# Wd loaded early into the rows of Wk and Wv, row normalisation allowed on GpSimd, and a new unit order, in a linear-attention block with a bilinear MLP

## The chip, the cores and the metric

The kernel runs on one core of one Trainium2 chip. The metric is the device time in microseconds (us). Kernels that are compared were run on the same chip in the same rounds as the kernel before.

## The reference, cut to what matters

```python
x = A_x                                     # 1 x 2048 x 640, bf16
h  = x + attn(layernorm(x)) ; out = h + mlp(layernorm(h))

def attn(x):                                # H = 32 heads of 20
    q, k, v = split(x @ wqkv)
    phi(t)  = concat(softmax(t @ w_phi), softmax(-(t @ w_phi)))
    kv = phi(k)^T v ;  z = sum over s of phi(k)
    o  = (phi(q) kv) / (phi(q) z + 1e-6)
    return o @ wo
def mlp(x):                                 # F = 1536
    return ((x @ w_gate) * (x @ w_up)) @ w_down
```

There are 16 row tiles of 128 rows. Each is normalised, transposed and projected to K and V; all sixteen must have gone into `kv` before any `o` is made.

## The kernel before

The program is a graph of named units. Unit `xn5` normalises row tile 5, `K5` and `V5` are its projections, `KV5` its key-value product, `wd0` a piece of the load of `w_down`. A table gives each unit a key and, sometimes, an alternative engine. A list scheduler orders the units on each engine with estimated costs; each engine then runs its own list strictly in order, with semaphores between the engines. So a unit that waits holds up everything behind it on its engine.

The statistics of a row tile give a mean `mv`, a reciprocal deviation `rs` and a bias `nb = -mean * rs`. VectorE normalises with mean and deviation; ScalarE needs the bias instead. The bias is made on GpSimd, for every tile from 2 on:

```python
for t in tl:
    if t > 1:
        G.op("pool", "L1n%d" % t, lambda e, t=t: e.tensor_scalar(
            out=T["nb"][:, t:t + 1], in0=T["mv"][:, t, 0:1], scalar1=T["rs"][:, t:t + 1], scalar2=-1.0,
            op0=ALU.mult, op1=ALU.mult), 0.2, LP, [rs_b[t], mv_b[t]], [nb_b[t]], 10 * t - 25)
# ... cut ...
def xn(e, eng="dve", t=t, xb=xb):
    if eng == "act":
        return e.activation(out=rev(xb), in_=..., func=AF.Identity,
                            scale=T["rs"][:, t:t + 1], bias=T["nb"][:, t:t + 1])
    return e.tensor_scalar(out=rev(xb), in0=..., scalar1=T["mv"][:, t, 0:1], scalar2=T["rs"][:, t:t + 1],
                           op0=ALU.subtract, op1=ALU.mult)
G.op("dve", "xn%d" % t, xn, 0.5, LD, [x_b[t], mv_b[t], rs_b[t], nb_b[t]], [xb], 10 * t - 22,
     alts=[] if t < 2 else [("act", act_c(640, True), LA)])
```

The unit lists `nb_b[t]` among what it reads whichever engine runs it. VectorE's form does not use the bias and waits for it all the same.

The cost that the scheduler assumes for any GpSimd operation of n columns, and the load of Wd, which lies over the first twelve of the fifteen row tiles of the weights of Q, K and V and so waits for the last projection:

```python
def pool_c(n):
    return 0.183 + 0.0017 * n
# ... cut ...
for k in range(4):
    dma("sp", "wd%d" % k, lambda k=k: T["Wd"][:, 3 * k:3 * k + 3, :], ..., 492, [wd_b[k]], key=310,
        after=lastproj)
```

The softmax here doesn't subtract the row's maximum and nothing guards it: scores larger than these inputs give would overflow.

## Time and profile before

| what | before |
|---|---|
| median, and range of 3 runs | 282.76 us, 282.46 to 282.84 |
| span of the profiled execution | 281.1 us |
| first real matmul starts, last ends | 5.59 us, 278.53 us |
| TensorE busy from 15.5 to 50 us | all of 34.5 us |
| normalisation on VectorE, ScalarE, GpSimd | 11, 5, 0 tiles |

The main lines of the page are in the prediction. Beside them, the views of single source lines show what the units in question cost; each gives engine, operation, tiles and count, then the shortest, median and longest duration in ns, and the first and last start in us. Here are the normalisation on VectorE and on ScalarE, the bias on GpSimd, and the only other row operation of 640 columns that GpSimd does, a product of two inputs.

```profile
L442 DVE TENSOR_SCALAR xn<-x_all,mv,rs x11: 589/597/605, 5.3 to 41.6; 128x640 bf16<-128x640 bf16 x11
...
L440 ACT ACTIVATE xn<-x_all,nb,rs x5: 910/921/959, 14.0 to 38.8; 128x640 bf16<-128x640 bf16 x5
...
L421 POOL TENSOR_SCALAR nb<-mv,rs x14: 262/267/268, 13.2 to 40.8; 128x1 f32<-128x1 f32 x14
...
L599 POOL TENSOR_TENSOR scratch<-scratch,sm x10: 1271/1272/1277, 88.6 to 218.2; 128x640 bf16<-128x640 f32 x10
```

### The profile page before, as it was taken

How to read it: one execution, taken by the hardware profiler on the slowest of the kernel's cores; microseconds unless marked ns; L12 is line 12 of the kernel's file. 1: busy time of each engine (PE TensorE's matmuls, PEld its weight loads, DVE VectorE, ACT ScalarE, POOL GpSimd, SP SyncE). 2: the span in 40 equal slices, each digit the busy share in tenths (PEclk: the TensorE clock that was granted, in tenths of full speed). 3: DMA queues.
4: the chain of work that ended last, by engine and by line, in shares of the span. 5: the costliest groups of instructions: out<-in, count | busy, mean ns of one | idle time of the engine just before them, and what ended most of it. 6: DMA issues, size and time to landing. Idle time of an engine off the chain costs nothing.

```text
span 281.1 us, 5047 instructions
## 1 busy us (share of the span) xinstructions
PE 274.9 (98%) x2058; PEld 182.7 (65%) x2075; DVE 176.8 (63%) x357; ACT 109.6 (39%) x217; POOL 61.3 (22%) x78
## 2 busy tenths in 40 slices
PE   7899999999999999999999999999999999999996
PEld 3677777876556688765555675545675554587874
DVE  5899986542588798855888974338725452341532
ACT  3799876846785742112311301303200203330200
POOL 6017998873002102202012000010110200000000
PEclk9999999999999999999999999999999999999999
DMA  7923276990011692232111342010141230000001
GB/s 211 369 56 74 53 131 113 313 372 8 0 26 31 153 261 48 41 79 49 25 23 26 70 106 60 0 23 2 25 97 47 40 32 23 0 2 23 26 34 60
DMA packets 43479, 21.98 MB, mean 78 GB/s; under 512 B 34624, under 2 KB 42176, under 8 KB 43456
## 3 DMA queue, kind: packets, MB, share of 16 engines
q1 hardware_dynamic: 42080, 20.02, 28.9%
q10 hardware_dynamic: 1376, 1.64, 1.9%
q8 instruction: 16, 0.26, 0.4%
q14 instruction: 7, 0.06, 0.1%
HBM read 11.00 MB, written 2.62 MB: 48 GB/s over the span
## 4 chain that ended last, share of the span: by engine, by line
PE 95%; DMA 2%; DVE 1%; issue 0%; ACTq 0%; ACT 0%; POOL 0%; DVEq 0%
PE ps L652 36%; PE ps L671 19%; PE ps L473 16%; PE ps L610 8%; PE ps L534 8%; PE ps L567 4%; PE ps L513 4%; DMA scratch<-in_A_wqkv_dram 2%; PE ps L389 1%; PE ps L370 0%; PE ps L451 0%; DVE x_all L614 0%; DVE ev L660 0%; DVE st L620 0%; ACTq L274 0%
## 5 line engine op out<-in xcount | busy, mean ns | idle before, releaser
L652 PE MATMUL ps<-xnT,Wgu 128*128 128x512 bf16 (+1 forms) x587 | 106.4, 335 | 0.7
L652 PEld LDWEIGHTS ps<-xnT,Wgu 128*128 128x128 bf16 x600 | 58.1, 98 | 41.7 <-DVE ev L660 0.6
L657 ACT ACTIVATE scratch<-ps 128x512 bf16<-128x512 f32 (+1 forms) x60 | 30.7, 512 | 117.4 <-PE ps L652 98.5
L660 DVE TENSOR_TENSOR ev<-ps,scratch 128x512 bf16<-128x512 f32 (+1 forms) x60 | 33.6, 579 | 34.5 <-ACT scratch L657 18.7
L671 PE MATMUL ps<-Wp,ev 128*128 128x320 bf16 (+2 forms) x396 | 53.5, 295 | 0.0
L671 PEld LDWEIGHTS ps<-Wp,ev 128*128 128x128 bf16 x396 | 38.0, 98 | 14.1
L473 PE MATMUL ps<-Wp,xnT 128*128 128x320 bf16 x320 | 45.9, 299 | 0.0
L504 POOL TENSOR_TENSOR ev<-ev,SR 128x1280 bf16<-128x1280 bf16 x16 | 37.4, 2358 | 9.5 <-ACT SR L502 9.5
L473 PEld LDWEIGHTS ps<-Wp,xnT 128*128 128x128 bf16 x320 | 30.7, 98 | 11.2
L599 POOL TENSOR_TENSOR scratch<-scratch,sm 128x640 bf16<-128x640 f32 x10 | 12.7, 1273 | 94.9 <-DVE sm L596 91.7
L683 DVE SCALAR_TENSOR_TENSOR Wp<-ps,rs,x_all 128x640 bf16<-128x640 f32 (+3 forms) x18 | 14.5, 808 | 30.0 <-PE ps L671 30.0
L497 DVE TENSOR_REDUCE SR<-ev 128x64 f32<-128x1280 bf16 x16 | 23.3, 1475 | 6.2 <-ACT ev L494 6.1
L610 PE MATMUL ps<-Wo,scratch 128*128 128x320 bf16 x160 | 24.0, 299 | 0.0
L543 ACT ACTIVATE eqT<-ps 128x512 bf16<-128x512 f32 x40 | 21.4, 598 | 6.2 <-PE ps L534 6.2
L494 ACT ACTIVATE ev<-ps 128x640 bf16<-128x640 f32 x32 | 21.6, 713 | 4.2 <-PE ps L473 3.6
L534 PE MATMUL ps<-xnT,Wp 128*128 128x512 bf16 x96 | 21.9, 379 | 0.2
L610 PEld LDWEIGHTS ps<-Wo,scratch 128*128 128x128 bf16 x160 | 15.6, 98 | 7.0 <-issue 0.2
L614 DVE TENSOR_TENSOR x_all<-ps,x_all 128x640 bf16<-128x640 f32 x16 | 12.9, 813 | 7.8 <-PE ps L610 7.8
L534 PEld LDWEIGHTS ps<-xnT,Wp 128*128 128x128 bf16 x100 | 9.6, 98 | 10.3
L567 PE MATMUL ps<-KVm,eqT 128*128 128x154 bf16 (+1 forms) x192 | 15.7, 221 | 0.0
L567 PEld LDWEIGHTS ps<-KVm,eqT 128*128 128x128 bf16 x192 | 13.0, 98 | 4.0
L624 POOL TENSOR_SCALAR ln<-mv 128x1 f32<-128x1 f32 x16 | 3.3, 210 | 49.4 <-DVE mv L623 47.3
(59 smaller groups left out, 204.4 us busy)
## 6 DMA issues: line engine op xcount, KB each, us to landing
out_dram<-Wp SPq DMA_DIRECT2D x15, 160.0 KB, 1.8
x_all<-in_A_x_dram SPq DMA_DIRECT2D x6, 320.0 KB, 10.0
Wgu<-in_B_w_up_dram SPq DMA_DIRECT2D x5, 384.0 KB, 7.7
Wgu<-in_B_w_gate_dram SPq DMA_DIRECT2D x5, 384.0 KB, 6.1
Wp<-in_B_w_down_dram SPq DMA_DIRECT2D x4, 480.0 KB, 5.2
scratch<-in_A_wqkv_dram ACTq DMA_DIRECT2D x2, 320.0 KB, 5.5
Wo<-in_A_wo_dram SPq DMA_DIRECT2D x1, 480.0 KB, 9.0
xnT<-xn SPq DMA_TRANSPOSE x28, 2.7
```

The lines of the kernel that those rows point to most:

```text
L473: ins = e.matmul(pb(b, hb)[:, 0:320], lhsT=T["xnT"][:, NC - 1 - c, P * t:P * (t + 1)], rhs=T["Wp"][:, kind, c, 320 * hb:320 * (hb + 1)], s ...
L494: G.op("act", "Kx%d_%d" % (t, s), lambda e, s=s, b=b, ek=ek: e.activation(out=T["ek"][:, ek.slots[0], s, :].rearrange("p (b n) -> p b n", ...
L497: G.op("dve", "Ks%d" % t, lambda e, ek=ek, sr=sr: e.tensor_reduce(out=T["SR"][:, sr.slots[0], 0, :], in_=T["ek"][:, ek.slots[0], :, :].rea ...
L504: G.op("pool", "Kn%d" % t, lambda e, ek=ek, sr=sr: e.tensor_tensor(out=T["ek"][:, ek.slots[0], :, :].rearrange("p s (h f) -> p (s h) f", f ...
L534: ins = e.matmul(pb(b)[:, 0:n], lhsT=T["Wp"][:, 0, i, P * c:P * (c + 1)], rhs=T["xnT"][:, NC - 1 - i, o0:o0 + n], start=(i == 0), stop=(i ...
L543: G.op("act", "Qx%d_%d_%d" % (q, c, s), lambda e, s=s, c=c, o0=o0, n=n, b=b: e.activation(out=T["eqT"][:, s, c, o0:o0 + n], in_=pb(b)[:, 0 ...
L567: ins = e.matmul(pb(b, y)[:, 22 * h0:22 * (h0 + j1 - j0)], lhsT=T["eqT"][:, s, c, P * t:P * (t + 1)], rhs=T["KVm"][:, OFF[s, c] + j0:OFF[s ...
L610: ins = e.matmul(pb(b, hb)[:, 0:320], lhsT=T["oT"][:, oT.slots[0], c, :], rhs=T["Wo"][:, c, 320 * hb:320 * (hb + 1)], start=(c == 0), stop ...
L652: ins = e.matmul(pb(b)[:, 0:n], lhsT=T["Wgu"][:, gu, c, P * ft:P * (ft + 1)], rhs=T["xnT"][:, NC - 1 - c, o0:o0 + n], start=(c == 0), stop ...
L657: G.op("act", "g%d_%d" % (bi, ft), lambda e, pg=pg, gt=gt, n=n: e.activation(out=T["gt"][:, gt.slots[0], 0:n], in_=pb(pg)[:, 0:n], func=AF ...
L660: o_ = G.op("dve", "u%d_%d" % (bi, ft), lambda e, pu=pu, gt=gt, hh=hh, ft=ft, n=n: e.tensor_tensor(out=T["hh"][:, hh.slots[0], ft, 0:n], i ...
L671: ins = e.matmul(pb(b, hb)[:, 0:w], lhsT=T["hh"][:, hh.slots[0], ft, P * tt:P * (tt + 1)], rhs=T["Wd"][:, ft, c0 + w * hb:c0 + w * (hb + 1 ...
```

## The change

It has three parts. Wd is laid out so that ten of its twelve row tiles lie over Wk and Wv, and may load while Q is being computed. Normalisation gets GpSimd as a third choice. And a new table of keys was searched with these freedoms; it puts tiles 4, 5 and 11 on GpSimd, 7 and 14 on ScalarE, the rest on VectorE.

```diff
+WDP = [(0, 3), (3, 5), (5, 8), (8, 10), (10, 12)]
 TUNED = {}                                  # about 170 lines of keys, replaced as a whole; cut
+def wdc(f):
+    return 5 + f if f < 10 else f - 10
@@ bias
-            if t > 1:
+            if t not in TPE:                # TPE = (0, 1, 2, 3)
@@ normalisation
-             alts=[] if t < 2 else [("act", act_c(640, True), LA)])
+             alts=[] if t in TPE else [("act", act_c(640, True), LA), ("pool", pool_c(640), LP)])
@@ load of Wd
-    for k in range(4):
-        dma("sp", "wd%d" % k, ... T["Wd"][:, 3 * k:3 * k + 3, :], ..., 492, [wd_b[k]], key=310, after=lastproj)
+    for k, (f0, f1) in enumerate(WDP):
+        own = lastproj if f0 >= 10 else [o for o in projs if o.name[0] == ("K" if f0 < 5 else "V")]
+        dma("sp", "wd%d" % k, ... T["Wd"][:, wdc(f0):wdc(f0) + WDN[f0], :], ..., 164 * (f1 - f0), [wd_b[k]], key=310, after=own)
@@ down matmul
-    rhs=T["Wd"][:, ft, ...]
+    rhs=T["Wd"][:, wdc(ft), ...]
@@ scheduler's estimate of a load: two constants changed; place of the output rows moved; cut
```

Every matmul stays, in shape and in number.

## The prediction

> **What bounds the kernel now.** I read the page first: busy time by engine, the 40 slices, then the costliest groups. TensorE is busy nearly all of the time; no other engine passes two thirds.
>
> ```profile
> PE 274.9 (98%) x2058; PEld 182.7 (65%) x2075; DVE 176.8 (63%) x357; ACT 109.6 (39%) x217; POOL 61.3 (22%) x78
> PE   7899999999999999999999999999999999999996
> PEclk9999999999999999999999999999999999999999
> ```
>
> The first slice and the last are the only ones with room, and the clock is full throughout. But a busy TensorE is not yet a TensorE at its own rate, so I took the cadence from the chain that ended last, in order of time.
>
> ```profile
> 8.41 0.73 PE ps L370 x10
> ...
> 15.52 15.21 PE ps L473 x112
> 30.73 1.36 PE ps L513 x24
> ...
> 195.25 3.24 PE ps L652 x15
> ...
> 265.45 13.08 PE ps L671 x108
> ```
>
> 15.21/112 is 0.136 us for a matmul of 320 columns, 3.24/15 is 0.216 us for 512 columns, 1.36/24 is 0.057 us for the small ones of the key-value product. Elsewhere in that chain 256 columns go at 0.109 us (1.64/15), six numerator matmuls in 0.36 us, one fold of six in 0.32 us, a transpose of five in 0.28 us.
>
> Now the work, counted in the source. Gate and up: 360 of 512 columns and 240 of 256, 77.8 + 26.2 = 104.0 us. Down: 372 x 0.136, plus 12 of 192 and 12 of 128 columns (about 0.083 and 0.056 each), 52.2. K and V: 320 x 0.136 = 43.5. Q: 100 x 0.216 = 21.6. Output projection: 160 x 0.136 = 21.7. Numerators 32 x 0.36 = 11.4, key-value 16 x 0.68 = 10.9, folds 10 x 0.32 = 3.2, transposes 9 x 0.28 = 2.5. The sum is **271.0 us**. The first real matmul starts at 5.59 us and the last ends at 278.53, which is 272.9 us. So in the whole stream TensorE loses about **1.9 us**, 0.2 of it a warm-up matmul. The waits of TensorE say where:
>
> ```profile
> PE ps L370 <- DMA scratch<-in_A_wqkv_dram: 1.4, 2, 1.1
> PE ps L349 <- DVE zero L344: 1.2, 1, 1.2
> ```
>
> Its one long wait is for the second piece of Wk (until 8.41 us); after that the list has nothing. The chain shows one stretch of VectorE and GpSimd, 219.66 to 222.69 us, but the timeline has 19 matmuls of 512 columns running from 219.46 on, so it is no hole. The limits, then: a head of 5.6 us (launch, first DMA), 1.9 us of loss, 271.0 us of matmuls, and a tail of 281.1 - 278.5 = 2.5 us (last combination and output write).
>
> **What the Trainium skill says.** "Perfetto Trace Analysis", Identifying the Most-Contended Engine, warns that matmul busy share is a bad measure of headroom. This case agrees that it can't be used alone: one 512-column matmul is recorded as 379 ns but follows the last by 216. Hence the sum by cadence. "TensorE: Matmul & The Clock Gate", Back-to-back issue gap, gives N/2.4 + 2.5 ns for an isolated matmul and 131 ns at N=512 as sustained. The trace has 216 ns, which is the formula and not the sustained figure. "GPSIMD Engine Reference", 3.1 Elementwise, puts GpSimd at about 1.8 to 2.6 cycles an element, the upper one for two inputs; the two-input product of 640 columns on GpSimd took 1.27 us here (820 ns on VectorE), in line. "DMA: Bandwidth & Descriptors", Issuing engines are not separate DMA queues, says that all transfers share the same 16 engines, so moving the Wd load moves what it may disturb.
>
> **The change, part by part.** Every matmul stays: same shapes, same count. So TensorE's 271.0 us stay, and only the 1.9 us, the head and the tail can move.
>
> (1) Wd. Before, four pieces of 480 KB are issued at 94.9 to 96.8 us, because Wd takes the place of Wq, Wk and Wv and must wait for the last Q matmul. They move at 340 to 400 GB/s and land at about 103 us.
>
> ```profile
> 94.84 1.36 PE ps L610 x10
> ...
> 115.88 6.52 PE ps L671 x48
> ```
>
> The first down matmul comes at 115.88 us, so the load was hidden with 13 us to spare. Now ten of twelve row tiles go into the rows of Wk and Wv and may start after the last K and V projection, about 62 to 67 us, and the last two after Q. The loads of Wgu and Wo stop near 63 us (372 GB/s in the slice to 63, then 8, 0, 26), so the lanes are free. At some 370 GB/s the 1.6 MB need 4.4 us (an estimate) and end before the first transposes of o near 79 us. Worth on the path: **0**. It frees the time from 95 to 103 us of DMA traffic; the transposes there take 2.9 us against a usual 2.6 to 2.7, hidden too.
>
> (2) Normalisation on GpSimd. The new order puts three of the sixteen (tiles 4, 5, 11) on GpSimd and two on ScalarE (five before); VectorE keeps eleven. ScalarE saves 3 x 0.92 = 2.8 us; GpSimd gains 3 x about 1.2 = 3.6 (an estimate between the page's one-input rate, 640 x 1.8 / 1.2 GHz = 0.96 us, and the measured 1.27) and loses two bias operations of 0.27. These engines are crowded where it happens, 14 to 42 us:
>
> ```profile
> 14.00:28.00 14.00, 14.00 (x112) 10.24 (x110) 14.00 (x32) 13.51 (x31) 6.10 (x7) 1.00 0.31 66
> 28.00:42.00 14.00, 14.00 (x141) 11.03 (x139) 13.03 (x21) 11.53 (x27) 14.00 (x14) 1.00 0.45 90
> ```
>
> (Columns: TensorE, weight loads, VectorE, ScalarE, GpSimd busy, clock, DMA.) VectorE and GpSimd are full, and yet TensorE is busy for all 14.00 us. Relief of an engine that TensorE does not wait for is worth **0**. It helps the search for an order, not this time.
>
> (3) The new order of units. At the start the DMA issues up to the sixth x load are the same, so the second Wk piece should land at about 8.4 us again. In front of that wait TensorE has the same amount to do (two weight transposes, one x transpose, one fold). Behind it the fold of chunk 0 now comes first, so its copy on ScalarE comes later, and the copies of chunks 0, 3 and 2 (0.70 us each) queue there in front of K's third chunk. With the trace's durations I get about 0.45 us of gaps between 8.4 and 13.6 us, where before has 7.11 us elapsed less 6.76 us of matmuls by cadence = 0.35 us up to 15.52. Cost: **0 to +0.2 us**.
>
> In the middle I looked at the tight places. K15 to its key-value product: about 6.3 us of chain (two exponentials 1.36, reduction 1.48, logarithm and exponential 0.53, product on GpSimd 2.36, hand-overs 0.5) against 7.7 us of matmuls placed between. The end of O0 to the first gate matmul: some 6.4 us (addition 0.82, statistics 1.1, centring 0.82, transpose 2.7, hand-overs) against 7.1 us placed between, where the old order left 7.8. Both hold, the second with 0.7 us only. I add **+0.1** for such places.
>
> At the end the last piece is 128 columns wide, not 192: the combination takes 343 ns in place of 418, and the output of 32 KB about as long as 48 KB (1.6 and 1.5 us). Worth **-0.1**.
>
> Sum: 0 + 0 + 0.1 + 0.1 - 0.1, about 0.1 us, less a little for the likelihood that an order was kept because it ran well. From 282.76 I stay at **282.7 us**.
>
> **The rivals.** First, the start gains: if the order cut all the loss, it would save at most 1.7 us (1.9 less the warm-up), giving 281.1. For it: all the loss is there. Against it: the wait is for a transfer whose issue is unchanged. Second, a new wait in TensorE's in-order queue: a fixed order tuned on estimates may block on a late transpose or a GpSimd product. GpSimd is full from 28 to 42 us and now gets more there; a slip of 1 to 3 us would give 284 to 286. Against it: the old order, made the same way, lost nothing after 15.5 us. Third, the early Wd load collides with a transpose or the last Wgu pieces. Those are first read near 96 us, 30 us later, so it should be hidden; time 282.7. Fourth, freed ScalarE speeds things: no TensorE wait names ScalarE; 282.7.
>
> **Range and chances.** To be faster by 2% means 5.7 us, which is more than loss, idle start and tail offer without removing a matmul: 0.01. To be slower by 2% needs 5.7 us of new stalls: 0.02. The rest, 0.97, is within. Range 281.7 (half of the early loss gone) to 283.8 (one new stall of about a microsecond).
>
> **What will show it.** Right: TensorE about 98% busy, the last matmul ending near 278.5 us, no wait of TensorE after 16 us, the same wait for the Wk piece until about 8.4. Wd issues near 64 to 69 us and one near 97, none of them in the list of waits. GpSimd busy about 64 us, ScalarE about 107. Wrong: if the Wk piece lands at another time; if TensorE's list names a transpose, a GpSimd product or a Wd transfer; if normalisation on GpSimd takes far over 1.3 us and K4, K5 or K11 wait for it.

## The result, and the profile after

| what | before | after |
|---|---|---|
| median, and range of 4 runs each | 282.68 us, 282.46 to 282.84 | 285.33 us, 285.2 to 285.44 |
| ratio, with 95% interval | | 1.0094, 1.0077 to 1.0112 |
| span of the profiled execution | 281.1 us | 283.7 us |
| first real matmul starts, last ends | 5.59, 278.53 us | 5.57, 281.26 us |
| normalisation on VectorE, ScalarE, GpSimd | 11, 5, 0 tiles | 11, 2, 3 tiles |

Ratios here and below are the mean time of one kernel's fast runs over that of the other's of the same rounds, so not quite the ratio of the medians that are quoted. The changed kernel is slower by 0.9%: within 2%, but 1.5 us beyond the predicted range.

From the first matmul to the last it takes 275.7 us, where before took 272.9: 2.8 us more. The tail behind the last matmul is 0.13 us shorter (2.44 against 2.57), so nearly all of the 2.6 us of span is TensorE's. The busy line of the page, against the first line of the prediction:

```profile
PE 276.2 (97%) x2075; PEld 182.4 (64%) x2075; DVE 179.4 (63%) x359; ACT 107.3 (38%) x214; POOL 66.2 (23%) x77
```

GpSimd is at 66.2 us where about 64 was predicted. That looks like a near hit and is not one, as the last part shows. The waits of TensorE have new entries; each line gives who was waited for, then us in total, times, and the longest.

```profile
PE ps L377 <- DMA scratch<-in_A_wqkv_dram: 1.3, 2, 0.9
...
PE ps L480 <- ACT ev L245: 1.2, 1, 1.2
PE ps L480 <- DVE ev L245: 0.8, 2, 0.5
```

The first is the old wait for the second piece of Wk. The other two are K and V projections (line 480) waiting for a copy out of PSUM (`ps`, where the results of the matmuls land), on ScalarE once and on VectorE twice; two waits of 0.2 us on ScalarE are left out here. By the order of units in the source the four late ones are K6, K4, K9 and K12, and each waits for a slot of PSUM, not for its own row tile. Neither says GpSimd. The table by stage says where: columns as in the prediction, the busy us of TensorE, weight loads, VectorE, ScalarE and GpSimd, then clock, DMA share and GB/s.

```profile
14.00:28.00 14.00, 12.59 (x98) 8.74 (x96) 11.96 (x24) 11.16 (x25) 10.59 (x9) 1.00 0.31 69
28.00:42.00 14.00, 13.55 (x128) 10.30 (x127) 11.76 (x24) 9.77 (x26) 14.00 (x11) 1.00 0.31 61
42.00:50.00 8.00, 7.64 (x78) 5.95 (x76) 6.64 (x7) 5.22 (x11) 8.00 (x8) 1.00 0.75 122
```

Before, the third of these stages was

```profile
42.00:50.00 8.00, 8.00 (x87) 6.44 (x85) 5.27 (x5) 5.39 (x13) 5.98 (x3) 1.00 0.73 113
```

and the first two stand in the prediction. TensorE loses 1.41, 0.45 and 0.36 us in these stages, 2.2 us together, and nothing that matters behind them. VectorE and ScalarE are less busy than before (11.96 against 14.00, 11.16 against 13.51, from 14 to 28 us): they wait too. GpSimd is busier, 10.59 against 6.10. The remaining 0.6 us hides in the records: a matmul of 320 columns is recorded as 299 ns but follows the last by 136, so each of the four gaps is some 0.16 us longer than it looks.

The chain that ended last, in order of time (start, us, what), confirms it. Before, it stays on TensorE from 15.52 us on, but for the short stretch near 220 us that the prediction tells of; now it lies almost wholly on GpSimd from 17.41 to 46.31 us.

```profile
17.41 0.74 POOL nb L428 x3
18.15 5.00 POOL xn L449 x2
23.15 0.24 POOL nb L428
23.39 9.26 POOL ev L511 x4
...
33.36 2.48 POOL xn L449
...
47.58 2.88 PE ps L480 x20
```

Two normalisations take 5.00 us. The view of that source line, with the median in the middle:

```profile
L449 DVE TENSOR_SCALAR xn<-x_all,mv,rs x11: 552/598/607, 5.3 to 47.9; 128x640 bf16<-128x640 bf16 x11
L449 POOL TENSOR_SCALAR xn<-x_all,mv,rs x3: 2499/2507/2525, 18.1 to 33.3; 128x640 bf16<-128x640 bf16 x3
```

The same operation takes 0.60 us on VectorE and **2.51 us on GpSimd**, twice the 1.2 that the prediction and the 1.27 that the scheduler's formula (0.183 + 0.0017 x 640) gave it. How this reaches TensorE is in the timeline around 23 us (start, us, engine, line, operation, and in brackets the idle time before it and its releaser):

```profile
18.13 5.02 POOL L449 TENSOR_SCALAR xn<-x_all,mv,rs 128x640 bf16<-128x640 bf16 x2
...
23.13 0.27 POOL L428 TENSOR_SCALAR nb<-mv,rs 128x1 f32<-128x1 f32 x1
...
23.43 0.92 ACT L447 ACTIVATE xn<-x_all,nb,rs 128x640 bf16<-128x640 bf16 x1 [2.42 <-POOL nb L428]
...
24.25 0.68 ACT L245 ACTIVATE ev<-ps 128x640 bf16<-128x640 f32 x1
...
24.99 1.53 PE L480 MATMUL ps<-Wp,xnT 128*128 128x320 bf16 x10 [1.23 <-ACT ev L245]
```

The bias for tile 7, a quarter of a microsecond of work, stands in GpSimd's list behind the two long normalisations. ScalarE idles 2.42 us for it, because the normalisation of tile 7 is next in *its* list. A copy out of PSUM stands behind that, and TensorE needs the slot which that copy frees. Three engines in a row, and the list of TensorE's waits names only the last hand. The later stalls are of the same family. VectorE's reduction at 38.50 us waited 0.77 us for a product on GpSimd, and the copy behind it, at 40.02, released TensorE at 40.94. VectorE's normalisation at 43.31 us waited 2.51 us for a bias that stood behind products on GpSimd, and the copy behind that, at 46.62, released TensorE at 47.58 us. VectorE's own operations are not slower beside the long ones: its normalisation has a median of 598 ns (597 before), its reduction a mean of 1476 ns (1475 before). So it was late, not slowed.

That is the reading of one trace. What it does not tell is which part is the cause: the long operation, the crowded list, the bias, or the order as such.

### The profile page after: what moved, and what is told of

Same layout as the page of the kernel before. It is cut to its first block, busy times and chain, and to the rows that moved or that the text cites. A ratio compares the mean times of both kernels' runs of the same rounds, so it can differ in the third digit from the quotient of the medians.

```text
span 283.7 us, 5057 instructions
## 1 busy us (share of the span) xinstructions
PE 276.2 (97%) x2075; PEld 182.4 (64%) x2075; DVE 179.4 (63%) x359; ACT 107.3 (38%) x214; POOL 66.2 (23%) x77
## 4 chain that ended last, share of the span: by engine, by line
PE 85%; POOL 10%; DMA 2%; ACT 1%; DVE 0%; issue 0%; ACTq 0%; DVEq 0%
PE ps L660 37%; PE ps L679 18%; PE ps L618 8%; PE ps L541 8%; PE ps L480 7%; POOL ev L511 7%; PE ps L575 4%; POOL xn L449 3%; DMA scratch<-in_A_wqkv_dram 2%; PE ps L520 2%; PE ps L396 1%; POOL nb L428 1%; ACT ev L501 1%; PE ps L377 0%; DVE ev L245 0%
## 5 line engine op out<-in xcount | busy, mean ns | idle before, releaser
L660 PE MATMUL ps<-xnT,Wgu 128*128 128x512 bf16 (+1 forms) x600 | 108.6, 336 | 0.0
L480 PE MATMUL ps<-Wp,xnT 128*128 128x320 bf16 x320 | 46.6, 299 | 2.2 <-ACT ev L245 1.2
L504 DVE TENSOR_REDUCE SR<-ev 128x64 f32<-128x1280 bf16 x16 | 23.4, 1476 | 5.4 <-ACT ev L501 4.6
L607 POOL TENSOR_TENSOR scratch<-scratch,sm 128x640 bf16<-128x640 f32 x8 | 10.2, 1272 | 60.4 <-DVE sm L604 60.4
L541 PE MATMUL ps<-xnT,Wp 128*128 128x512 bf16 x100 | 23.0, 379 | 0.0
```

Of the source, the lines that this page charges most:

```text
L480: ins = e.matmul(pb(b, hb)[:, 0:320], lhsT=T["xnT"][:, NC - 1 - c, P * t:P * (t + 1)], rhs=T["Wp"][:, kind, c, 320 * hb:320 * (hb + 1)], s ...
L504: G.op("dve", "Ks%d" % t, lambda e, ek=ek, sr=sr: e.tensor_reduce(out=T["SR"][:, sr.slots[0], 0, :], in_=T["ek"][:, ek.slots[0], :, :].rea ...
L541: ins = e.matmul(pb(b)[:, 0:n], lhsT=T["Wp"][:, 0, i, P * c:P * (c + 1)], rhs=T["xnT"][:, NC - 1 - i, o0:o0 + n], start=(i == 0), stop=(i ...
L660: ins = e.matmul(pb(b)[:, 0:n], lhsT=T["Wgu"][:, gu, c, P * ft:P * (ft + 1)], rhs=T["xnT"][:, NC - 1 - c, o0:o0 + n], start=(c == 0), stop ...
```

## The experiments

**Theory T**: the two-operation form of `TENSOR_SCALAR` takes 2.51 us on GpSimd, and this alone, through GpSimd's in-order list, delays TensorE. **Rivals**: the new order is slow by itself (R1); the early load of Wd disturbs something (R2); GpSimd is slow only because other engines use the memory at the same time (R3). In the expectations, "Theory A" is T, B is R1 and C is R2. In the experiments that move a unit, all other lists keep their order, and the unit goes to the same point in time on another engine's list:

```python
def _move(names, eng):                      # order[e]: the finished list of engine e
    for n_ in names:
        o_ = G.by[n_]
        order[o_.eng].remove(o_)
        o_.eng = eng
        insert o_ into order[eng] before the first unit with a later start
```

### 1. Only the normalisations, put into the old kernel

```diff
 # kernel before
+_move(["xn4", "xn5", "xn11"], "pool")
```

> The kernel before with only the normalisations of tiles 4, 5 and 11 put on GpSimd, at the same places in time. Theory A: GpSimd is full from 22 to 48 us there too, so 2.5 us each push the key-value products and bias operations back: 283.5 to 286 us with new TensorE waits between 20 and 50 us. Theories B and C: 282.7, no new wait.

Measured: 285.52 us (285.39 to 285.62) against 282.51, ratio 1.0107 (1.009 to 1.0124). The old order, with the old load of Wd, loses 3.0 us by this one part. Its list of TensorE's waits:

```profile
PE ps L473 <- DMA xnT<-xn: 1.5, 1, 1.5
...
PE ps L389 <- ACT SR L502: 0.7, 1, 0.7
```

The long operations run at 17.91 us, 5.01 us for two, and here TensorE waits for a transposed tile. So the loss needs neither the new order nor the early Wd, and R1 and R2 are not needed for a loss of this size. Where TensorE ends up waiting depends on the order; how much is lost is about the same.

### 2. The normalisations taken off GpSimd in the new kernel, to VectorE

```diff
 # kernel after
+_move(["xn4", "xn5", "xn11"], "dve")
```

> The changed kernel with the three normalisations (tiles 4, 5, 11) moved from GpSimd back to VectorE, everything else in the same order. Theory A (GpSimd needs 2.5 us for each where 1.2 was reckoned, and the bias operations and key-value products queue behind): the stalls of TensorE at 23.5 and 40 to 47 us go, 282.4 to 283.2 us. Theory B (the new unit order itself has the stalls): stays at 285.0 to 285.5. Theory C (the early Wd load disturbs): stays at 285.3.

Measured: 284.32 us (283.86 to 285.28) against 282.51, ratio 1.0069 (1.0044 to 1.0095). A quarter of the loss goes, not all: less than T had led me to expect (282.4 to 283.2 us). The waits for copies out of PSUM are gone, but there is a new one:

```profile
PE ps L480 <- DMA xnT<-xn: 1.0, 1, 1.0
```

It lies at 46 us. VectorE was busy for all of 14.00 us from 14 to 28 us in this run and runs late. The chain that ended last leads back from that tile to VectorE, and lies on it nearly all the way from 35.0 back to 11.9 us. This is not a clean undo: it puts 1.8 us on an engine that has no room there, and so it does not separate T from R1. A cleaner test had to keep the lists and change only the duration (run 7).

### 3. What the operation costs, form by form

Sixteen extra GpSimd operations were added at the end of the kernel before, two of each form, each waiting for the last one. They ran from 226.7 to 257 us, where VectorE is much less busy (4.14 of 13.00 us from 232 to 245) than in the crowd.

```diff
 # kernel before, end of GpSimd's list; M, X: 128 x 640 bf16; MR, XC: the same in five chunks, MR reversed
+2 x tensor_scalar(out=MR, in0=XC, mean, rstd, subtract, mult)      # L986, as in the change
+2 x tensor_scalar(out=M,  in0=X,  mean, rstd, subtract, mult)      # L988, no reversal
+2 x tensor_scalar(out=M,  in0=X,  0.5, 2.0, subtract, mult)        # L990, constants
+2 x tensor_scalar(out=MR, in0=XC, rstd, mult)                      # L992, one operation
+2 x tensor_scalar(out=M,  in0=X,  2.0, mult)                       # L994
+2 x tensor_tensor(out=MR, in0=XC, in1=rstd broadcast, mult)        # L996, two inputs
+2 x tensor_scalar(M[:, 0:320], X[:, 0:320], mean, rstd, subtract, mult)  # L998
+2 x tensor_copy(out=M, in_=X)                                      # L1000
```

> The kernel before with sixteen extra row operations of 640 columns on GpSimd after its last real work (about 226 us), two of each form, each waiting for the last: the normalisation as in the change; without the reversed order of chunks; with constants in place of the two per-row scalars; with one operation in place of two; with one operation and a constant; a two-input product with the row scalar broadcast; the normalisation of 320 columns; a plain copy. If two operations in one instruction are what costs, the one-operation forms take about 1.3 us and the two-operation forms 2.5 whatever the pattern; if the reversed order or the per-row scalars cost, the forms without them drop to about 1.3; if it was contention beside VectorE, the first form is well under 2.5 us here.

Measured (one look): the groups by line on GpSimd, with busy us and the mean ns of one.

```profile
L986 POOL TENSOR_SCALAR mb<-x_all,mv,rs 128x640 bf16<-128x640 bf16 x2 | 5.0, 2511 | 0.2
L988 POOL TENSOR_SCALAR mb<-x_all,mv,rs 128x640 bf16<-128x640 bf16 x2 | 5.0, 2500 | 0.2
...
L994 POOL TENSOR_SCALAR mb<-x_all 128x640 bf16<-128x640 bf16 x2 | 3.6, 1808 | 0.2
...
L998 POOL TENSOR_SCALAR mb<-x_all,mv,rs 128x320 bf16<-128x320 bf16 x2 | 2.9, 1432 | 0.2
L996 POOL TENSOR_TENSOR mb<-x_all,rs 128x640 bf16<-128x640 bf16 x2 | 2.5, 1252 | 0.2
L1000 POOL COPY mb<-x_all 128x640 bf16<-128x640 bf16 x2 | 1.4, 718 | 0.1
```

Away from the crowd it takes the same 2.51 us, so R3 falls as far as VectorE, ScalarE and the DMA go (TensorE was as busy there as in the crowd, 13.00 of 13.00 us). The reversed chunks cost nothing (2.50). The two row scalars cost 0.15 us over constants (L990, 2.35). One operation in place of two still takes 1.81 to 1.88 us. The **two-input product takes 1.25 us** and a copy 0.72. So none of the three explanations is enough by itself: from 2.50 down to 1.25 us the row scalars make up 0.15 and the second operation 0.54 to 0.63, and the rest goes with the instruction itself. From 320 to 640 columns the form grows by 1.07 us, 3.3 ns a column, over a fixed 0.36 us.

The skill's "GPSIMD Engine Reference", 4.1 Engine selection, says that with one input GpSimd is "roughly line-rate" and with two about half as fast as VectorE. For the copy that fits roughly (0.72 us, where VectorE's copies of 640 columns out of PSUM took 0.77 to 0.82 us in the changed kernel). For `TENSOR_SCALAR` the measurement reverses it: the form with one tensor input costs twice the product with two, so the number of tensor inputs was the wrong guide to the price, and the measurement decides.

### 4. All biases taken off GpSimd, the normalisations left on it

```diff
 # kernel after; ten of twelve biases are read by nobody
-L1n4, 5, 6, 8, 9, 10, 11, 12, 13, 15 on pool
+_move(["L1n7", "L1n14"], "dve")
```

> The changed kernel with the three normalisations still on GpSimd, but the bias operations taken from its queue: the ten that no ScalarE normalisation needs are left out, the two for tiles 7 and 14 are made on VectorE. If the stalls come through the bias operations (ScalarE at 23.4 us, VectorE at 36 and 43 us waited for them), 283 to 284 us and no stall at 23.5 us; if through late key-value products or late transposes alone, 285 to 285.5 us.

Measured: 283.33 us (282.71 to 283.49) against 282.16, ratio 1.0035 (1.0019 to 1.0051). The stall that ended at 24.99 us is gone, and so are the later ones; one wait of the middle is left:

```profile
PE ps L520 <- POOL ev L511: 0.7, 1, 0.7
```

It is the key-value product (line 520), at 26.54 us, waiting for GpSimd itself. So about two thirds of the loss (0.94% down to 0.35%; the intervals are 0.77 to 1.12 and 0.19 to 0.51) went with the biases, and the rest fits the products that GpSimd finishes late. That all of the two thirds travelled by a *wait for a bias* is not shown: the twelve biases are also some 3.2 us of work (12 x 0.27) taken from GpSimd's list. For the stall that ended at 24.99 us the trace of the changed kernel shows the bias as the link.

### 5. The normalisations to ScalarE

```diff
 # kernel after
+_move(["xn4", "xn5", "xn11"], "act")
```

> The changed kernel with the three normalisations on ScalarE (0.92 us each) in place of GpSimd. Theory A: like the run with them on VectorE or better, 282.7 to 284.3 us, as ScalarE has room (9.8 of 14 us busy between 28 and 42). If the order itself is at fault: 285 us.

Measured: 283.48 us (282.81 to 284.09) against 282.16, ratio 1.0052 (1.0033 to 1.007). The waits of TensorE have one for a transposed tile left, 0.6 us; ScalarE was busy 12.32 of 12.50 us from 15.5 to 28 us. As in run 2, an engine with no room takes over part of the loss.

### 6. VectorE, and no biases on GpSimd

```diff
 # kernel after
+_move(["xn4", "xn5", "xn11"], "dve"); _move(["L1n7", "L1n14"], "dve")
-the ten biases that nobody reads
```

> The changed kernel with the normalisations on VectorE and also no needless bias operation on GpSimd. If what is left of the loss after the first experiment (284.3 us, one TensorE wait for a transposed tile at 45 us) comes from the bias operation of tile 14 behind a key-value product, 282.5 to 283.3 us; if it is the order's own tightness, 284 us again.

Measured: 284.33 us (283.39 to 285.81) against 282.16, ratio 1.0079 (1.0042 to 1.0117). The wait of 1.0 us for a transposed tile is still there. The idea that a late bias (tile 14) caused it in run 2 has fallen, and the time is what the expectation gave to the order's own tightness; run 7 tests that. Three extra normalisations on a full VectorE are the likely reason. The traces agree as far as they go: as in run 2, the chain leads back along VectorE, and the three transposes of row tiles that begin at 32.00 us in run 12, with one of the three on VectorE, begin at 33.06 us in run 2 and 32.92 us here. No run was made to test it.

### 7. The same lists, a shorter operation (wrong result)

The three normalisations stay on GpSimd, in the same place of the same list, with the same waits, but as the two-input product of 1.25 us. It leaves the mean in, so the result is wrong (relative error 0.050).

```diff
 # kernel after
+if eng == "pool": return e.tensor_tensor(out=rev(xb), in0=x, in1=rstd broadcast, op=ALU.mult)
 return e.tensor_scalar(out=rev(xb), in0=x, scalar1=mean, scalar2=rstd, op0=ALU.subtract, op1=ALU.mult)
```

> The changed kernel with the GpSimd normalisation of tiles 4, 5 and 11 replaced by a two-input product of the row with its scale, which took 1.25 us alone where the two-operation form took 2.5. The mean is not taken off for these three tiles, so the result is wrong on purpose (it may still pass). Nothing else moves. If the duration of that one instruction is the cause of the loss, 282.3 to 283.3 us and no TensorE wait between 20 and 48 us; if the new order itself is too tight, 284 us or more.

Measured: 282.22 us (281.68 to 282.29) against 282.44, ratio 0.9978 (0.9952 to 1.0004). The three took 1.25 us each; TensorE waits nowhere after the start. By stage:

```profile
14.00:28.00 14.00, 14.00 (x122) 10.53 (x121) 14.00 (x30) 12.86 (x30) 11.27 (x10) 1.00 0.29 58
28.00:42.00 14.00, 14.00 (x137) 10.91 (x135) 12.13 (x17) 9.93 (x25) 14.00 (x15) 1.00 0.47 84
```

TensorE is busy for all of both stages again, with GpSimd as full as in the changed kernel (11.27 and 14.00 us against 10.59 and 14.00). This is the deciding run: new order, early Wd, every list and every wait as in the changed kernel, only the form, and with it the duration, of three instructions differs, and the whole loss is gone. T stands, and R1 and R2 fall. The trace is that of the fastest of the four, with the second piece of Wk used early, at 7.38 us; the other three took 282.18 to 282.29 us. The run also shows that the order fits the cost it was planned with: at about 1.25 us it runs as well as the old one.

### 8. Early Wd alone, in the old kernel

```diff
 # kernel before
-WDP of four pieces over rows 0 to 11, after the last projection
+ten of twelve row tiles over Wk and Wv, after the last K or V projection; two after Q
```

> The kernel before with only the Wd change: ten row tiles into the rows of Wk and Wv after the last K and V projections, two after Q, orders of all compute engines untouched. Theory A and the prediction: 282.7 (within 0.3), the loads land near 75 us and nobody waits. Theory C: slower by 1 us or more.

Measured: 282.23 us (281.73 to 283.0) against 282.51, ratio 0.9985 (0.9962 to 1.0008): no difference shown. But one line did change. Before, the transposes of o land after

```profile
DMA to landing us min/median/max: 2.6/2.6/8.0
```

and here the longest is 4.3. The one of 8.0 us was issued at 96.88 us, right behind the pieces of Wd in the same queue, and landed at 104.9; the first weight load of its output projection began at 105.00 and the first matmul at 105.11. The prediction called this "hidden" with 2.9 us; it was hidden with about 0.1 us to spare.

### 9. The new kernel with Wd late

```diff
 # kernel after; wd0 to wd3 wait for the last Q matmul too, issued 98.4 to 101.0 us
-wd0..wd3 after their own K or V projections
+wd0..wd3 after all of K, V and Q, in front of wd4
```

> The changed kernel with all five Wd pieces issued only after the last Q matmul, near 97 us, as before. Theory A and B: 285.3 (within 0.3), since the load is hidden at either time. Theory C: back towards 282.7.

Measured: 288.62 us (287.34 to 289.51) against 282.51, ratio 1.0214 (1.0173 to 1.0255): slower, but whether by more than 2% is unclear. I had expected 285.3 and missed by more than three microseconds. The list of TensorE's waits is led by

```profile
PE ps L618 <- DMA scratch<-scratch: 3.0, 1, 3.0
```

a transpose of o that took 7.57 us (102.31 to 109.88 us) behind Wd. In this order its output projection comes too early to hide that. And the idle time costs twice, as the table by stage shows: the clock column, third from the right, falls after it.

```profile
106.00:110.00 4.00, 1.02 (x10) 0.67 (x9) 1.93 (x5) 0.00 (x0) 1.27 (x1) 0.94 0.93 124
110.00:113.00 3.00, 3.00 (x13) 1.73 (x14) 0.19 (x1) 0.00 (x0) 0.00 (x0) 0.51 0.29 55
113.00:116.00 3.00, 3.00 (x27) 2.45 (x26) 2.71 (x7) 0.97 (x3) 0.21 (x1) 1.00 0.00 0
```

Ten matmuls of 320 columns and five of 256 took 3.39 us there (109.92 to 113.31) in place of 1.91 by the usual cadence, so 3.0 us of waiting brought 1.5 us more. Not in every run: two of the four had a mean clock of 0.994 and took 289.5 us, the other two (0.999 and 1.0) took 287.34 and 287.74. Only one of the four has a trace, so the gap in the others is not known; it seems to lie at the edge of what the clock bears. This agrees in kind with "TensorE: Matmul & The Clock Gate", What's actually happening, which has the clock halve after an idle window of about 3.4 us and recover after a busy one. Here the clock stood at 0.51 for the 3 us after the gap and was back at 1.00 in the next 3; the gap itself was recorded as 2.98 us, a little less than the page's window. The stalls at 23 to 48 us of the changed kernel, 1.4 us at most, left the clock at 1.00.

### 10. Wd later still, behind the transposes

```diff
 # kernel after
-wd0..wd3 after their own projections
+wd0..wd4 behind the transpose of o of tile 4, issued 110.9 to 113.6 us
```

> The changed kernel with all Wd pieces issued behind the transpose of o for tile 4, near 108 us, so that they stand ahead of no transpose that is needed soon. In the run with the late load one transpose took 7.6 us behind the Wd pieces and TensorE waited 3.0 us for it. If the order in the queue is what cost, 285 to 286 us; if the load has to be over early for another reason (bandwidth, the first down matmul at 119 us), 287 us or more.

Measured: 286.47 us (285.99 to 289.43) against 282.44, ratio 1.0155 (1.0111 to 1.0199), between the two ranges. The transpose is out of trouble (4.1 us at most), but the first down matmul now waits:

```profile
PE ps L679 <- DVE sm L590: 1.4, 1, 1.4
```

By the source, this matmul does not need the unit at line 590 that the list names; what it needs of VectorE (line 668) had ended at 117.96 us. What came in time for the start at 120.04 us was the last piece of Wd, issued at 113.1 and landed 6.7 us later, at 119.8: the releaser that the list names is the wrong one. Of the two late places tried in the new order neither is good: behind the last Q Wd delays a transpose, behind that transpose it comes late itself. One of these runs, too, had a clock of 0.994, and it is the one of 289.43; the other three took 285.99 to 286.66. Going by the ratios less 1.0094, early Wd is worth 0.6% and 1.2% of 282.5, or 1.7 and 3.4 us, to the *new* order, against these two places; without the three runs at 0.994 it is some 1.1 and 2.4 us. To the old order no worth is shown.

### 11. The start

Most of the 1.9 us that TensorE loses before is at the start. The first loads were issued in another order, to bring the second piece of Wk sooner.

```diff
 # kernel before, first loads of both issuing queues (ScalarE; SyncE), same times of issue
+ScalarE: x1 wk0 wv0 wv2 wv4 x4
+SyncE:   w5 x0 wk2 wk4 x2 x6 x14
```

> The kernel before with the first loads in another order: the second Wk piece goes to the SyncE queue right behind the first x tile, the x tiles 2 to 5 behind the weights, all Wv pieces on the ScalarE queue. Nothing else moves. By the bytes ahead of it in its queue the Wk piece should land about 2 us sooner. If the 1.1 us wait of TensorE for it is what is left to gain, 281.3 to 282.0 us, about 1 us faster than before; if the x tiles then come late, the same as before or slower.

Measured: 283.34 us (283.21 to 283.86, 6 runs) against 282.44, ratio 1.0027 (1.0003 to 1.005). A miss. TensorE used its Wk piece at 8.28 us, against 8.41 in the trace of the kernel before, and then waited 0.4 us for a normalised tile whose x came later. But 8.41 is one look, and a poor measure: with the old first loads the piece was used at 7.61 us in run 1 and 8.47 in run 8 (one chip), and at 7.37 in run 3, on the chip of this run. So no gain is shown even for the piece itself. The loads share the same DMA engines, which were full there in the kernel before (DMA share 1.05 from 5.6 to 8.4 us); that what is moved forward makes something else late is the likely reason.

### 12. The best mix

```diff
 # kernel after
+_move(["xn4"], "dve"); _move(["xn5", "xn11"], "act")
-the eight biases that nobody reads then
```

> A correct repair of the changed kernel: normalisation of tile 4 on VectorE, of 5 and 11 on ScalarE, none on GpSimd, and the eight bias operations that no ScalarE normalisation needs left out; the early Wd load and the new order stay. From the run with the fast product (282.2 us, level with before) this should come to 282.0 to 282.8 us, no TensorE wait between 16 and 50 us: as fast as before, not faster by more than 0.3%, since the matmuls are the same 271 us.

Measured: 282.58 us (282.08 to 284.12, 6 runs) against 282.58, ratio 1.0006 (0.998 to 1.0032), with the right result. Nothing of the list of waits lies between 16 and 50 us, and by stage:

```profile
14.00:28.00 14.00, 14.00 (x117) 10.16 (x115) 14.00 (x31) 13.39 (x30) 7.10 (x5) 1.00 0.30 64
```

The loss is repaired with no trick, and no gain appears. No version that I ran beats the kernel before; the 271.0 us of matmuls were in all of them.

## Why the prediction was right or wrong, point by point

**The bound** held. TensorE sets the time, its matmuls kept their 271.0 us, and each microsecond that came or went in a run was a wait of TensorE or, once, its clock. The class, within 2%, held; the range (281.7 to 283.8) did not.

**The step that failed** is part (2): "GpSimd gains 3 x about 1.2 = 3.6 (an estimate between the page's one-input rate ... and the measured 1.27)", followed by "Relief of an engine that TensorE does not wait for is worth **0**". Two things are wrong in it. The size: 3 x 2.51 = 7.5 us, shown in the trace and, alone, in run 3. The prediction priced a two-operation `TENSOR_SCALAR` by a `TENSOR_TENSOR` of the same columns, and the page gives its 1.8 cycles as the best case of a tight loop, not as the rate of an operation with one input. And the sign: the part was weighed only as relief of ScalarE, while it was also a *load* on GpSimd, whose list holds small units that others wait for. That engine was shown as full from 28 to 42 us in the prediction's own table; but the longest stall came where it was not (6.10 of 14.00 us from 14 to 28 before), for a bias stood there behind 5 us of work in one piece. At 1.25 us the load is worth 0, as the step says (run 7); at 2.51 us it costs about 2.7 us (285.33 less 282.68).

**The rival** that came true was the second: a slip of 1 to 3 us in an in-order list, "284 to 286". It had the size and the kind of mechanism, a block in an in-order list. The place, from 28 to 42 us, holds for 0.45 of the 2.2 us only (1.41 were lost from 14 to 28), and the wait reached TensorE by copies out of PSUM and not by a transpose or a GpSimd product. It was set aside because "the old order, made the same way, lost nothing after 15.5 us". That the old order had been planned with true costs (its GpSimd products take 1.27 and 2.36 us, as the formula says) says nothing of an order that uses an operation nobody had timed; the old order with that operation loses 3.0 us (run 1). The list of what would be wrong named this too, "far over 1.3 us"; that "K4, K5 or K11 wait for it" did not come true in that form.

**Part (1), Wd**, was right for the kernel as it was: worth 0 in the old order (run 8), and in the new kernel no Wd piece appears in the waits; it was issued at 66.4 to 70.6 and 98.95 us, close to the 64 to 69 and 97 foretold. But "the transposes there take 2.9 us against a usual 2.6 to 2.7, hidden too" rested on a median over a stretch; one transpose took 8.0 us. And part (1) was judged alone. With the new order, a late Wd costs more in both places tried (runs 9 and 10): the early load is part of what lets that order run.

**Part (3), the order**, held in its terms: Wk was used at 8.16 us (8.41 before; no gain, as the time moves between 7.4 and 8.5 us from one execution to the next, see run 11), the tail gained 0.13 us where 0.1 was foretold, and the tight places that I had computed by hand did not stall. "No wait of TensorE after 16 us" failed, for part (2)'s reason.

**The checks.** ScalarE at 107.3 us hit the 107. GpSimd at 66.2 against about 64 seems to support 1.2 us an operation, but it does not: three at 2.51 us add 7.5, two biases fewer take 0.5, and the new order moved two of ten output products (1.27 us each, so 2.5) to VectorE, with 0.5 more in a small unit of the second normalisation (line 632, 3.8 against 3.3 us). 61.3 + 7.5 - 0.5 - 2.5 + 0.5 = 66.3. A total can agree while a term of it is off by a factor of two.

**What stays open.** Why the form costs 3.3 ns a column was not measured; a full VectorE as the origin of the wait for a transposed tile in runs 2 and 6 is likely from the traces, and not tested; and how the two thirds of run 4 divide between waits for a bias and work taken off GpSimd is open. That the search chose GpSimd because its formula said 1.27 us is likely from the source, but no run tests it.

## What to carry to other kernels

Before an operation moves to another engine, time that very form there: the price of a similar one (a product in place of a two-operation scalar form) was wrong by a factor of two, and so was the planner's. In an in-order list, ask what small unit stands behind a long one and who waits for it; here it was a 0.27 us bias, most often needless, and with the biases off GpSimd's list about two thirds of the loss were gone. Of a wait that is hidden, look at the longest and not at the median, and compare it with the slack of the one that uses it.

## What the Trainium skill lacked or had wrong

- "GPSIMD Engine Reference", 3.1 Elementwise and 4.1 Engine selection: nothing there prices `TENSOR_SCALAR`, and one-input work is called roughly line-rate. At 128 x 640 bf16 the runs show 2.50 us with two operations and row scalars, 2.35 with constants, 1.81 to 1.88 with one operation, against 1.25 for the two-input product and 0.72 for a copy. VectorE took 0.60 us for the two-operation form, so GpSimd is 4.2 times slower there.
- "TensorE: Matmul & The Clock Gate", Back-to-back issue gap: 131 ns at N=512 is given as sustained. Every long run of such matmuls in the trace has 216 ns, the figure that the section gives to an isolated one. (An earlier section of the page, Wait — 56ns, not 53.3ns?, does give 215.7 ns for back-to-back ones, and the trace agrees with that.)
- No page that I read gives the delay of a transpose that is issued behind bulk loads on the same queue: 8.0 us in the kernel before and 7.6 us in run 9, against a usual 2.6.
